# Four weight combinations prepared five rounds later, and three engines' work reordered at the start of a fused retention and mixture kernel

## The chip, the cores and the metric

The kernel runs on one core of a Trainium2 chip. The metric is the device time of one execution in microseconds (us). Engines: PE (matrix products), DVE (vector), ACT (scalar and copies), POOL (GpSimd, elementwise here) and SP, whose queue issues nearly all transfers.

## The reference, cut to what matters

```python
def _attn_ref(q, k, v):                    # B, H, S, D = 4, 8, 768, 64
    gamma = 1.0 - 2.0 ** (-5.0 - np.arange(H, dtype=np.float32))
    for t in range(S):
        state = gamma[None, :, None, None] * state + np.einsum('bhd,bhe->bhde', k[:, :, t], v[:, :, t])
        y[:, :, t] = scale * np.einsum('bhd,bhde->bhe', q[:, :, t], state)

def _moe_ref(x, domain_probs, w1, w2):     # N, D, E, F = 3072, 512, 4, 1024
    p = domain_probs / (domain_probs.sum(-1, keepdims=True) + 1e-09)
    for e in range(E):
        h = np.maximum(x @ w1[e], 0.0)
        out += p[:, e:e + 1] * (h @ w2[e])
```

All values are float32. The output of the retention, 768 tokens of 512 columns for each of four batches, is the input x of four experts, whose results are added with normalised weights p.

## The kernel before, in words

**Numbers in two parts.** A float32 factor of a product is held as a high part (a rounded copy in the type fp32r, made by ACT: `w1h`, `xh`, `hh`, `c2h`, `w2h`) and a low part (the factor minus its high part, made by DVE or POOL: `w1l`, `xl`, `hl`, `c2l`, `w2l`). A product is then three products on PE: high by high, high by low, low by high.

**Rounds.** The experts' hidden columns are worked off in 16 rounds for each batch (n = 0 to 15 for the first one, 64 in all). A round multiplies x by a 512x256 piece of w1. From n = 1 on it does so with seven products of half-size blocks in place of eight, in the order `SEQ = (1, 5, 6, 2, 7, 3, 4)`; this needs sums and differences of blocks of x (`t1`, `t2`, `t4`, and the block b12 of `xr`, which is overwritten) and of w1. The seven blocks of w1 lie in one tile, `w1h` and `w1l`: part 0 holds three raw blocks (columns 0 to 2), part 1 four combinations (columns 3 to 6, made by `combine_w1` in the tile `s`). The products collect in the banks ps_x, ps_y and ps_z; ACT copies intermediate sums out (`u`), DVE adds them (L434), ACT and DVE make the two parts of the relu (`hh`, `hl`, L448 and L449).

**Round 0** is done differently: `whole` (L541) multiplies plain blocks, with the three raw blocks of w1 in part 0 and the fourth one (`a21`, `a` in the profile). So the combinations of w1[0] are not used in round 0. They are used by the later batches, which fetch all seven blocks of each round from DRAM (`kept1`, stored by `save_w1`).

**The second product.** For the first batch p2 (L561) multiplies hidden values by w2, into two banks ps_o, which ACT empties in round 0 (L578) and DVE later (L580). For the other batches w2 is also combined (`combine_w2`, which overwrites the loaded tile `w2r`, giving `c2h` and `c2l`) and kept in DRAM. `w2r` is one tile: the load of the next w2 (L270) has to wait until the last reader, c2l, is done.

**The order is written out by hand**: each engine executes its instructions in the order of the code. The opening runs the six chunks of the first attention (L707 to L739), then the four `whole` products with the preparation of x and of round 1's weights between them (L740 to L777). Then comes the loop over rounds n and their seven products k = 0 to 6 (L781 on): at each k come product p1(n, i), one p2 of the round before, and `weights(n, k)` (L354), which prepares weights for round n + 1. In that function k = 0 does c2h of the round before and starts `combine_w1` of the next one on POOL, k = 1 does c2l and loads the next w2, k = 4 and 5 make w2h and w2l, k = 6 combines w2 on POOL. The steps of the next batch's attention are spread through the rounds. Tiles with few buffers tie the queues together: `w1r` has two, `s`, `w2r`, ps_y and ps_z one each.

Of the kernel before, what the change touches and what calls it, by code (L numbers as in the profile page):

```python
# [7 lines left out]
F32 = mybir.dt.float32  # L8
F32R = mybir.dt.float32r
ACTF = mybir.ActivationFunctionType  # L10
ALU = mybir.AluOpType
# [13 lines left out]
WARM = (384, 384, 384, 384)  # L25
NB0 = S // 128
NP = NRND // 2
ATT_STEPS = 2 * NCHB + 2


# [30 lines left out]
def retention_moe(ctx: ExitStack, tc: tile.TileContext, qk, kv, w1, w2, probs, probt, cst, cqs, out, out_t):  # L61
# [260 lines left out]
        eng.tensor_tensor(out=a12, in0=a12, in1=a11, op=ALU.subtract)  # L322

    def save_w1(n):
        for i, x in enumerate(wt1[n]):
            nc.sync.dma_start(out=kept1[n][:, :, i, :], in_=x.bitcast(F32))

    def save_w2(n, d, at, which=(0, 1), eng=None):
        for i in which:
# [24 lines left out]
    def weights(n, k):  # L354

        m = n + 1
        if k == 0:
            if n == 1:
                save_w1(1)
                x_lo(0, 4)  # L360
            hi2(n - 1, wc2, "c2")
            if m < NRND:
                load_w1(m + 1)
                combine_w1(m, nc.gpsimd)
                w1_hi(m, 0)
        elif k == 1:
            lo2(n - 1, wc2, nc.vector)
            load_w2(n)
            if m < NRND:
                w1_lo(m, 0, nc.gpsimd)  # L370
        elif k == 2:
            save_w2(n - 1, wc2, 4)
            if n == 3:
                gates()
        elif k == 3 and m < NRND:
            w1_hi(m, 1)
        elif k == 4:
            hi2(n, wt2, "w2")
            if m < NRND:
                w1_lo(m, 1, nc.gpsimd)  # L380
        elif k == 5:
            lo2(n, wt2, nc.vector if m < NRND else nc.gpsimd)
            if m < NRND:
                save_w1(m)
        elif k == 6:
            combine_w2(n, nc.gpsimd)
            if m < NRND:
                save_w2(n, wt2, 0)
            else:
                save_w2(n, wt2, 0, (0,), nc.scalar)  # L390
# [290 lines left out]
    with tc.manual_schedule():  # L681
# [25 lines left out]
        for ci in range(NCHB):  # L707
# [8 lines left out]
            if ci == 1:  # L716
                w1_hi(0, 0)
                first_a21(0)
                combine_w1(0, nc.gpsimd)
            elif ci == 2:  # L720
                w1_hi(0, 1)
                w1_lo(0, 0, nc.gpsimd)
            elif ci == 3:
                for i in SEQ:
                    x_tiles(0, i)
                for i in (1, 2):
                    x_hi(0, i)
                first_a21(1)
                first_gates()
            elif ci == 4:  # L730
                decay(ci + 1)
                w1_lo(0, 1, nc.gpsimd)
                w1_hi(1, 0)
                hi2(0, wt2, "w2")
                load_w1(2)
                load_qk(6)
                load_kv(6)
# [1 line left out]
                decay(ci + 1)  # L739
        start[0] = False  # L740
        early, late = slice(0, 2 * C), slice(2 * C, HB)
        x_lo(0, 1, eng=nc.gpsimd)
        for i in (7, 3):
            x_hi(0, i, early)
        x_lo(0, 7, early, nc.gpsimd)
# [5 lines left out]
            x_lo(0, i, late)  # L751
        combine_w1(1, nc.gpsimd)
        whole(*WHOLE[0])
        w1_hi(1, 1)
        w1_lo(1, 1, nc.gpsimd)
        w1_lo(1, 0, nc.gpsimd)
        for c in range(2):
            combine_x(0, c, nc.vector, None, 0)
        whole(*WHOLE[1])
        lo2(0, wt2, nc.vector)  # L760
        combine_x(0, 2, nc.vector, None, 0)
        x_hi(0, 5)
        whole(*WHOLE[2])
        x_hi(0, 6)
        x_lo(0, 5)
        whole(*WHOLE[3])
        x_lo(0, 6)
        for c in range(3):
            combine_x(0, c, None, nc.gpsimd, 1)
        for i in range(3):  # L770
            p2(0, i)
        for i in (7, 4):
            x_hi(0, i)
        x_lo(0, 7, eng=nc.gpsimd)
        combine_w2(0, nc.gpsimd)
        save_w1(0)
        save_w2(0, wt2, 0)  # L777

# [129 lines left out]
```

## Time and profile before

| what | value |
|---|---|
| device time, median of 3 runs | 1063.77 us (1063.53 to 1064.26) |
| profiled execution | 1063.8 us, of it the profile's span 1062.0 us |
| busy in the span | PE 98%, DVE 67%, POOL 64%, ACT 36% |
| mean granted clock of PE | 0.996 |
| HBM traffic over the span | 274 GB/s (read 221.64 MB, written 69.26 MB) |

Times in the profile count from the start of the span. A row of the timeline gives start, length, engine, line, operation, output<-inputs, shape, and in brackets how long the engine had been idle and what released it. SPq rows are the issue of a transfer by SP. The name `k` stands for tiles in DRAM.

### The profile page before, as it was taken

How to read it: one execution, taken by the hardware profiler on the slowest of the kernel's cores; microseconds unless marked ns; L12 is line 12 of the kernel's file. 1: busy time of each engine (PE TensorE's matmuls, PEld its weight loads, DVE VectorE, ACT ScalarE, POOL GpSimd, SP SyncE). 2: the span in 40 equal slices, each digit the busy share in tenths (PEclk: the TensorE clock that was granted, in tenths of full speed). 3: DMA queues.
4: the chain of work that ended last, by engine and by line, in shares of the span. 5: the costliest groups of instructions: out<-in, count | busy, mean ns of one | idle time of the engine just before them, and what ended most of it. 6: DMA issues, size and time to landing. Idle time of an engine off the chain costs nothing.

```text
span 1062.0 us, 18481 instructions
## 1 busy us (share of the span) xinstructions
PE 1045.1 (98%) x6714; PEld 993.7 (94%) x6714; DVE 713.6 (67%) x1181; ACT 379.1 (36%) x728; POOL 678.4 (64%) x643
## 2 busy tenths in 40 slices
PE   8889999999999999999999999999999999999998
PEld 6778888888888999999999999999999999999998
DVE  5757767667766467677588467667679746677664
ACT  2354333344444422322252532332234443323320
POOL 5977675866757664655579754655658865555561
PEclk9999999999999999999999999999999999999999
DMA  9689999998979777878778987877678887787873
GB/s 343 227 287 331 352 298 331 299 335 274 363 253 333 256 259 262 269 269 279 243 246 270 327 278 242 263 265 268 225 253 261 292 288 260 251 268 252 264 263 103
DMA packets 153883, 292.13 MB, mean 275 GB/s; under 512 B 12352, under 2 KB 76992, under 8 KB 153792
## 3 DMA queue, kind: packets, MB, share of 16 engines
q1 hardware_dynamic: 151872, 288.32, 81.0%
q10 hardware_dynamic: 1920, 2.62, 0.7%
q8 instruction: 54, 0.88, 0.3%
q14 instruction: 37, 0.30, 0.1%
HBM read 221.64 MB, written 69.26 MB: 274 GB/s over the span
## 4 chain that ended last, share of the span: by engine, by line
PE 88%; DVE 3%; POOL 3%; DMA 2%; issue 2%; ACT 2%; POOLq 0%; DVEq 0%; ACTq 0%
PE ps_u L598 31%; PE ps_x L521 23%; PE ps_z L521 12%; PE ps_o L572 9%; PE ps_y L521 6%; PE ps_s L149 2%; PE ps_v L196 2%; PE ps_u L617 1%; POOL xl L253 1%; DMA w1r<-in_w 1%; PE ps_v L190 1%; PE ps_v L163 1%; DMA w2r<-in_w 1%; DVE w2l L314 0%; DVE ol L461 0%
## 5 line engine op out<-in xcount | busy, mean ns | idle before, releaser
L598 PE MATMUL ps_u<-oh,v 128*128 128x384 f32 x1288 | 378.9, 334 | 0.3 <-DVE sum L434 0.3
L472 POOL TENSOR_TENSOR b<-b 128x384 f32<-128x384 f32 x184 | 196.3, 1067 | 176.7 <-DVE b L470 150.7
L434 DVE TENSOR_TENSOR sum<-ps_u,sum 128x384 f32<-128x384 f32 x288 | 158.3, 550 | 135.7 <-PE ps_u L598 122.6
L598 PEld LDWEIGHTS ps_u<-oh,v 128*128 128x128 f32 x1288 | 237.2, 188 | 1.0 <-DVE sum L434 0.7
L461 POOL TENSOR_TENSOR ol<-b,oh 128x384 fp32r<-128x384 f32 x188 | 197.7, 1070 | 61.3 <-ACT oh L456 55.1
L456 ACT ACTIVATE oh<-b 128x384 fp32r<-128x384 f32 x330 | 160.6, 518 | 208.0 <-DVE b L470 111.2
L521 PE MATMUL ps_x<-xh,v 128*128 128x384 f32 x768 | 227.5, 337 | 0.2
L598 PE MATMUL ps_u<-ol,v 128*128 128x384 f32 x644 | 215.2, 334 | 0.0
L428 ACT ACTIVATE u<-ps_x 128x384 f32<-128x384 f32 x126 | 61.8, 490 | 253.1 <-PE ps_x L521 252.1
L461 DVE TENSOR_TENSOR ol<-b,oh 128x384 fp32r<-128x384 f32 x142 | 130.2, 917 | 25.6 <-ACT oh L456 25.6
L521 PEld LDWEIGHTS ps_x<-xh,v 128*128 128x128 f32 x768 | 141.4, 188 | 3.0 <-ACT u L428 0.9
L521 PE MATMUL ps_x<-xl,v 128*128 128x384 f32 x384 | 128.4, 334 | 0.0
L598 PEld LDWEIGHTS ps_u<-ol,v 128*128 128x128 f32 x644 | 120.9, 188 | 0.0
L521 PE MATMUL ps_z<-xh,v 128*128 128x384 f32 x384 | 113.9, 337 | 1.2 <-DVE ol L461 1.2
L580 DVE SCALAR_TENSOR_TENSOR acc<-ps_o,pm,acc 128x512 f32<-128x512 f32 x90 | 67.0, 744 | 38.4 <-PE ps_o L572 38.3
L572 PE MATMUL ps_o<-w2h,hh 128*128 128x512 f32 x192 | 75.6, 394 | 5.1 <-ACT acc L578 5.1
L572 PE MATMUL ps_o<-w2h,hl 128*128 128x512 f32 x192 | 76.1, 396 | 0.0
L572 PE MATMUL ps_o<-w2l,hh 128*128 128x512 f32 x192 | 76.0, 396 | 0.0
L521 PEld LDWEIGHTS ps_z<-xh,v 128*128 128x128 f32 x384 | 70.7, 188 | 2.4 <-DVE b L470 1.5
L521 PEld LDWEIGHTS ps_x<-xl,v 128*128 128x128 f32 x384 | 72.1, 188 | 0.1
L521 PE MATMUL ps_z<-xl,v 128*128 128x384 f32 x192 | 64.2, 334 | 0.0
L521 PE MATMUL ps_y<-xh,v 128*128 128x384 f32 x192 | 56.9, 337 | 0.0
(123 smaller groups left out, 1663.8 us busy)
## 6 DMA issues: line engine op xcount, KB each, us to landing
v<-k SPq DMA_DIRECT2D x336, 256.0 KB, 3.2
v<-k SPq DMA_DIRECT2D x165, 512.0 KB, 4.2
k<-w1h SPq DMA_DIRECT2D x16, 896.0 KB, 7.0
k<-w1l SPq DMA_DIRECT2D x16, 896.0 KB, 7.0
qk<-in_qk SPq DMA_DIRECT2D x24, 512.0 KB, 5.4
kv<-in_kv SPq DMA_DIRECT2D x24, 512.0 KB, 5.8
w1r<-in_w SPq DMA_DIRECT2D x16, 512.0 KB, 7.0
w2r<-in_w SPq DMA_DIRECT2D x16, 512.0 KB, 4.3
```

Source lines behind the costliest of these rows:

```text
L149: nc.tensor.matmul(ps[r][:, p, :], lhsT=a[rows, 1, p, :], rhs=a[rows, 0, p, :], start=True, stop=True)
L163: nc.tensor.matmul(y[64 * r:64 * r + 64, p, :], lhsT=v[:, 0, h, :], rhs=v[:, 1, h, :], start=(bank is None), stop=True, skip_group_check=True,
L196: nc.tensor.matmul(ps[r][64 * k:64 * k + 64, half, :], lhsT=v[:, 1, h, :], rhs=sp[:, h, :], start=(c == 0 and half == 0), stop=True, skip_ ...
L428: nc.scalar.activation(out=t, in_=ps, func=ACTF.Copy)
L434: nc.vector.tensor_tensor(out=o, in0=ps, in1=u, op=ALU.add)
L456: nc.scalar.activation(out=hi, in_=t, func=ACTF.Copy)
L461: eng.tensor_tensor(out=lo, in0=t, in1=hi.bitcast(F32), op=ALU.subtract)
L472: sub = lambda o, a, b: nc.gpsimd.tensor_tensor(out=o, in0=a, in1=b, op=ALU.subtract)
L521: nc.tensor.matmul(ps, lhsT=lhsT[:, cs], rhs=rhs[:, kt, :], start=(fresh and m == 0), stop=(m == 5), skip_group_check=True,)
L572: nc.tensor.matmul(ps, lhsT=a[:, ts], rhs=b[:, fs, :], start=(m == 0), stop=(m == 5))
L580: nc.vector.scalar_tensor_tensor(out=acc[nt], in0=ps, scalar=sc, in1=acc[nt], op0=ALU.mult, op1=ALU.add)
L598: nc.tensor.matmul(ps, lhsT=w[:, r, l, ds], rhs=o, start=(m == 0), stop=(m == 5))
```

## The change

Five things are moved, and nothing is computed differently.

1. The combinations of w1[0] (four POOL operations), their high part on ACT and their low part on POOL leave the opening. `save_w1(0)` stores only the three raw blocks. In round `REST` = 5 w1[0] is loaded again (k = 2), combined on POOL (k = 5), and `rest_w1` (k = 6) makes the two parts block by block (ACT copy, POOL subtraction) and stores each. For the buffer that this takes, the load of w1[8] moves from k = 0 to k = 3 of round 6.
2. x1's low part moves on POOL from behind the attention to the place that the low part of w1[0]'s combinations had.
3. The first w2 low part moves from DVE to POOL, its combinations from POOL to DVE.
4. The second high part of x7 and that of x4 on ACT, the low part of x7 on POOL and the first c2h move from the end of the opening into round 1, k = 0 and 1.
5. The high and low parts of w1[1]'s combinations, and of t1 and t2 (x5, x6), are put behind later products; the first two p2 are issued ahead of x5's and x6's high parts.

Line numbers in the rows below differ by a few between the two kernels, as the change adds lines.

POOL at the end of the first attention and in what follows it, before (`yst` is the decay of the attention's state, `xl` a low part of x, `s` a combination of w1):

```order
L175 TENSOR_TENSOR yst_113<-yst_113,cst 128x256
L295 TENSOR_TENSOR w1l<-s,w1h 128x1024
L253 TENSOR_TENSOR xl<-xr,xh 128x768
L253 TENSOR_TENSOR xl<-xr,xh 128x2x256
L278 TENSOR_TENSOR s<-w1r 128x256
L279 TENSOR_TENSOR s<-s,w1r 128x256
L280 TENSOR_TENSOR s<-w1r,s 128x256
L281 TENSOR_TENSOR s<-w1r 128x256
L295 TENSOR_TENSOR w1l<-s,w1h 128x1024
L295 TENSOR_TENSOR w1l<-w1r,w1h 128x768
L222 TENSOR_TENSOR xr<-xr 128x2x128
```

and of the change:

```order
L176 TENSOR_TENSOR yst_113<-yst_113,cst 128x256
L254 TENSOR_TENSOR xl<-xr,xh 128x768
L254 TENSOR_TENSOR xl<-xr,xh 128x2x256
L279 TENSOR_TENSOR s<-w1r 128x256
L280 TENSOR_TENSOR s<-s,w1r 128x256
L281 TENSOR_TENSOR s<-w1r,s 128x256
L282 TENSOR_TENSOR s<-w1r 128x256
L315 TENSOR_TENSOR w2l<-w2r,w2h 128x1024
L296 TENSOR_TENSOR w1l<-s,w1h 128x1024
L296 TENSOR_TENSOR w1l<-w1r,w1h 128x768
L223 TENSOR_TENSOR xr<-xr 128x2x128
```

x1's low part follows the last decay directly; w2's low part of 1024 columns has come in between the combinations of w1[1] and their low parts.

ACT from the first p2 into round 1, before (`acc` empties a bank of p2, `xh<-t` and `xh<-xr` are high parts of x5, x6, x4 and x7, `u` empties a bank of p1):

```order
L249 ACTIVATE xh<-t_521 128x768
L448 ACTIVATE hh<-ps_h 128x384
L578 ACTIVATE acc<-ps_o,pm 128x512 x3
L249 ACTIVATE xh<-xr 128x768
L249 ACTIVATE xh<-t_522 128x768
L428 ACTIVATE u<-ps_x 128x384
L310 ACTIVATE c2h<-w2r 128x1024
L290 ACTIVATE w1h<-w1r 128x768
L428 ACTIVATE u<-ps_z 128x384
L578 ACTIVATE acc<-ps_o,pm 128x512
L428 ACTIVATE u<-ps_x 128x384
```

and of the change:

```order
L604 ACTIVATE acc<-ps_o,pm 128x512
L250 ACTIVATE xh<-t_512 128x768
L604 ACTIVATE acc<-ps_o,pm 128x512
L454 ACTIVATE u<-ps_x 128x384
L250 ACTIVATE xh<-xr 128x768
L291 ACTIVATE w1h<-w1r 128x768
L454 ACTIVATE u<-ps_z 128x384
L604 ACTIVATE acc<-ps_o,pm 128x512
L250 ACTIVATE xh<-t_513 128x768
L311 ACTIVATE c2h<-w2r 128x1024
L454 ACTIVATE u<-ps_x 128x384
```

c2h has moved behind the next round's part of w1h, a copy `u`, an `acc` and x4's high part, and x7's and x4's high parts behind the first `u`.

POOL at the end of round 5 and the start of round 6, of the change (before, `w2r` follows `w1l<-s` directly):

```order
L296 TENSOR_TENSOR w1l<-s,w1h 128x1024
L279 TENSOR_TENSOR s<-w1r 128x256
L280 TENSOR_TENSOR s<-s,w1r 128x256
L281 TENSOR_TENSOR s<-w1r,s 128x256
L282 TENSOR_TENSOR s<-w1r 128x256
L335 TENSOR_TENSOR w1c<-s,w1c 128x256 x4
L320 TENSOR_TENSOR w2r<-w2r 128x256
L321 TENSOR_TENSOR w2r<-w2r 128x256
L322 TENSOR_TENSOR w2r<-w2r 128x256
L323 TENSOR_TENSOR w2r<-w2r 128x256
```

Eight operations stand ahead of w2's combinations there. On ACT the four copies stand ahead of the first `u` of round 6; on SP the new load stands behind the store of c2l of round 5.

The diff:

```diff
     def save_w1(n):
+        p = slice(0, 7 if n else 3)
         for i, x in enumerate(wt1[n]):
-            nc.sync.dma_start(out=kept1[n][:, :, i, :], in_=x.bitcast(F32))
+            nc.sync.dma_start(out=kept1[n][:, p, i, :], in_=x[:, p].bitcast(F32))
+
+    def rest_w1():
+
+        for i in range(4):
+            t, u = v1_p.tile([128, 2, 256], F32R, tag="v1", name="w1c"), comb1[0][:, i, :]
+            nc.scalar.activation(out=t[:, 0, :], in_=u, func=ACTF.Copy)
+            nc.gpsimd.tensor_tensor(out=t[:, 1, :], in0=u, in1=t[:, 0, :].bitcast(F32), op=ALU.subtract)
+            nc.sync.dma_start(out=kept1[0][:, 3 + i], in_=t.bitcast(F32))
...
@@ weights(n, k), m = n + 1
         if k == 0:
             if n == 1:
                 save_w1(1)
-                x_lo(0, 4)
-            hi2(n - 1, wc2, "c2")
+                x_hi(0, 7)
+                x_lo(0, 7, eng=nc.gpsimd)
+                combine_w2(0, nc.vector)
+            if n > 1:
+                hi2(n - 1, wc2, "c2")
             if m < NRND:
-                load_w1(m + 1)
+                if n != REST + 1:
+                    load_w1(m + 1)
                 combine_w1(m, nc.gpsimd)
                 w1_hi(m, 0)
         elif k == 1:
+            if n == 1:
+                x_hi(0, 4)
+                x_lo(0, 4)
+                hi2(0, wc2, "c2")
             lo2(n - 1, wc2, nc.vector)
...
+            elif n == REST:
+                load_w1(0)
         elif k == 3 and m < NRND:
             w1_hi(m, 1)
+            if n == REST + 1:
+                load_w1(m + 1)
...
             if m < NRND:
                 save_w1(m)
+            if n == REST:
+                combine_w1(0, nc.gpsimd)
         elif k == 6:
+            if n == REST:
+                rest_w1()
             combine_w2(n, nc.gpsimd)
...
@@ the first attention, chunk ci
             if ci == 1:
                 w1_hi(0, 0)
                 first_a21(0)
-                combine_w1(0, nc.gpsimd)
             elif ci == 2:
-                w1_hi(0, 1)
                 w1_lo(0, 0, nc.gpsimd)
...
             elif ci == 4:
                 decay(ci + 1)
-                w1_lo(0, 1, nc.gpsimd)
+                x_lo(0, 1, eng=nc.gpsimd)
...
@@ behind the attention
-        x_lo(0, 1, eng=nc.gpsimd)
         for i in (7, 3):
             x_hi(0, i, early)
...
         combine_w1(1, nc.gpsimd)
         whole(*WHOLE[0])
+        lo2(0, wt2, nc.gpsimd)
+        for c in range(2):
+            combine_x(0, c, nc.vector, None, 0)
+        whole(*WHOLE[1])
         w1_hi(1, 1)
         w1_lo(1, 1, nc.gpsimd)
         w1_lo(1, 0, nc.gpsimd)
-        for c in range(2):
-            combine_x(0, c, nc.vector, None, 0)
-        whole(*WHOLE[1])
-        lo2(0, wt2, nc.vector)
         combine_x(0, 2, nc.vector, None, 0)
+        whole(*WHOLE[2])
+        whole(*WHOLE[3])
+        p2(0, 0)
         x_hi(0, 5)
-        whole(*WHOLE[2])
+        x_lo(0, 5)
+        p2(0, 1)
         x_hi(0, 6)
-        x_lo(0, 5)
-        whole(*WHOLE[3])
         x_lo(0, 6)
         for c in range(3):
             combine_x(0, c, None, nc.gpsimd, 1)
-        for i in range(3):
-            p2(0, i)
-        for i in (7, 4):
-            x_hi(0, i)
-        x_lo(0, 7, eng=nc.gpsimd)
-        combine_w2(0, nc.gpsimd)
+        p2(0, 2)
         save_w1(0)
         save_w2(0, wt2, 0)
```

More of the change, by code (lines that the diff above doesn't have):

```diff
@@ L27 @@
 NP = NRND // 2
+REST = 5
 ATT_STEPS = 2 * NCHB + 2
```

## The prediction, on record before the changed kernel ran

> **What bounds the kernel now.** I read the page's busy times first, then the busy time by stage, then what TensorE (PE) waited for, then each engine's rows in order of time between 20 and 70 us and around 115 to 145 us.
>
> ```profile
> PE 1045.1 (98%) x6714; PEld 993.7 (94%) x6714; DVE 713.6 (67%) x1181; ACT 379.1 (36%) x728; POOL 678.4 (64%) x643
> ...
> 20.00:30.00 10.00, 7.47 (x141) 5.97 (x137) 9.53 (x19) 5.16 (x8) 9.20 (x9) 1.00 0.89 302
> 30.00:40.00 10.00, 9.80 (x47) 9.80 (x48) 8.40 (x11) 1.98 (x3) 8.67 (x8) 0.83 0.61 215
> 40.00:50.00 10.00, 8.02 (x39) 6.63 (x38) 7.05 (x7) 6.03 (x10) 9.48 (x9) 1.00 0.91 288
> 50.00:60.00 10.00, 6.90 (x29) 5.90 (x28) 3.31 (x4) 5.12 (x9) 9.13 (x10) 0.88 0.22 46
> 60.00:70.00 10.00, 10.00 (x61) 9.14 (x61) 5.70 (x9) 4.26 (x7) 7.04 (x8) 0.95 1.06 367
> ```
>
> The columns are the stretch, its length, and the busy time of PE, its weight load, DVE, ACT and POOL, then the granted clock, DMA share and GB/s. PE is busy 98% of the span, and from 60 us on without a gap. Its own order is not changed by the edit, so it gains only by entering the steady rounds earlier, and loses only where it is made to stop. Of its 17 us without work, 7.8 us lie between 20 and 60 us, and there the clock is at 0.83 and 0.88 in two of the four stretches.
>
> ```profile
> PE ps_o L572 <- ACT acc L578: 5.1, 2, 3.1
> PE ps_h L555 <- POOL xl L253: 2.6, 1, 2.6
> PE ps_v L190 <- POOL yst L175: 1.1, 1, 1.1
> ...
> 30.20 0.64 PE L555 MATMUL ps_h<-xl,w1h 128*128 128x384 f32 x1 [2.63 <-POOL xl L253]
> 44.98 0.50 PE L572 MATMUL ps_o<-w2h,hh 128*128 128x512 f32 x1 [1.98 <-ACT acc L578]
> 56.71 0.50 PE L572 MATMUL ps_o<-w2h,hh 128*128 128x512 f32 x1 [3.10 <-ACT acc L578]
> 65.24 0.33 PE L521 MATMUL ps_z<-xh,w1h 128*128 128x384 f32 x1
> ...
> 31.00:32.00 1.00, 1.00 (x5) 1.00 (x4) 1.00 (x1) 0.00 (x0) 1.00 (x2) 0.50 1.09 381
> 59.00:60.00 1.00, 1.00 (x4) 1.00 (x4) 0.00 (x0) 1.00 (x2) 0.52 (x1) 0.50 0.73 280
> ```
>
> These are PE's waits (total, times, longest), four PE rows (start, length, in brackets the wait and what ended it) and two stretches of 1 us. PE waits 2.6 us for the low part of x1 from POOL, then 2.0 and 3.1 us for a bank that ACT empties. After the waits of 2.6 and 3.1 us the clock is at 0.50. A mean of 0.83 over 30 to 40 us is 3.4 us at half speed, and so are 0.88 and 0.95 over 50 to 70 us together: each costs PE 1.7 us more. After the wait of 2.0 us the clock stays up.
>
> What sets the end of this opening is the queue of POOL, and behind it a chain through w2:
>
> ```profile
> 26.92 1.13 ACT L249 ACTIVATE xh<-xr 128x512 fp32r<-128x512 f32 x2
> 27.63 4.20 POOL L253 TENSOR_TENSOR xl<-xr,xh 128x768 fp32r<-128x768 f32 x2
> 36.25 2.66 POOL L295 TENSOR_TENSOR w1l<-s,w1h 128x1024 fp32r<-128x1024 f32 x1 [1.17 <-ACT w1h L290]
> 45.50 1.45 POOL L222 TENSOR_TENSOR xr<-xr 128x256 f32<-128x256 f32 x1
> 47.26 0.84 ACT L249 ACTIVATE xh<-xr 128x768 fp32r<-128x768 f32 x1
> 53.91 1.06 ACT L310 ACTIVATE c2h<-w2r 128x1024 fp32r<-128x1024 f32 x1 [4.70 <-POOL w2r L322]
> 54.88 0.83 ACT L290 ACTIVATE w1h<-w1r 128x768 fp32r<-128x768 f32 x1
> 55.61 0.47 ACT L428 ACTIVATE u<-ps_z 128x384 f32<-128x384 f32 x1
> 55.98 0.68 ACT L578 ACTIVATE acc<-ps_o,pm 128x512 f32<-128x512 f32 x1
> 55.00 1.45 DVE L314 TENSOR_TENSOR c2l<-w2r,c2h 128x1024 fp32r<-128x1024 f32 x1 [4.17 <-ACT c2h L310]
> 56.48 0.35 SPq L270 DMA_DIRECT2D w2r<-in_w  x1
> 62.74 1.06 ACT L310 ACTIVATE w2h<-w2r 128x1024 fp32r<-128x1024 f32 x1 [0.71 <-DMA w2r<-in_w]
> 64.21 0.56 DVE L449 SCALAR_TENSOR_TENSOR hl<-ps_z,hh 128x384 fp32r<-128x384 f32 x1 [1.11 <-ACT hh L448]
> ```
>
> The third subtraction into b12 (xr<-xr) on POOL ends at 45.50 + 1.45 = 46.95, and ACT's second high part of x7 follows at 47.26. c2h waits 4.7 us for POOL's w2 combinations; its low part c2l ends at 56.45. Then w2r may be overwritten: the next load is issued at 56.48, its high part starts at 62.74. On ACT the relu of ps_z stands behind that high part, so hl<-ps_z ends at 64.77, and only then may the second product of round 2 write ps_z. PE does that at 65.24 without a wait.
>
> **The change, term by term.** Seen from the profiled execution of 1063.8 us (span 1062.0; the median of the three runs is 1063.77, so I use one for the other).
>
> *The attention.* POOL loses the four combinations of w1[0], which made PE's 1.1 us wait at ps_v; what is late next there are loads, which do not move. Between nothing and 1.1 us I take 0.8. x1's low part loses the low part of 1024 columns ahead of it (2.40 us by the row at 125.46 below) and these 0.8, so it ends near 27 or sooner and not as PE starts at 30.20. The wait of 2.6 us and its halved clock go, and PE ends the four whole products 4 to 5 us earlier.
>
> *That is not carried through.* POOL's long run begins with x7's early low part, which waits for ACT's high part. That is the first of the two in the row at 26.92, and it ends at 27.5; it stands behind a w1 load that does not move. Of old the run began when x1's low part ended, at 30.2, and reached 46.95 with one wait of 1.17 us: 15.6 us of work. New in it is w2's low part.
>
> ```profile
> 310.76 2.41 POOL c2l L314
> 34.98 0.41 DVE L222 TENSOR_TENSOR t<-xr 128x256 f32<-128x256 f32 x1
> 39.91 2.06 DVE L222 TENSOR_TENSOR t<-xr 128x256 f32<-128x256 f32 x1
> ```
>
> The first row is a subtraction of the same size that POOL does late in the program (2.41 us). So x7's second high part can start at 27.5 + 15.6 + 2.4 + 0.3 (the step from 46.95 to 47.26) = 45.8 instead of 47.26. PE, which came early, gives back some 1.5 us where round 1 needs w1[1]'s second low part from this same run. The other two rows are one DVE operation on 128x256 with POOL idle and with POOL busy: 0.41 and 2.06 us. The four w2 combinations, never seen on DVE, cost there 4 x 0.41 = 1.6 to 4 x 2.06 = 8.2 us; I take 3, nearer to the idle row, since POOL was slower beside such work but seldom by much (2.66 for 2.40 at 36.25). They follow x6's low part, and ACT wants them 3 us after x7, so they hide unless they take over 8 us. Their cost to POOL lies between nothing and their own 1.6 us; I take 0.2, as DVE also loses a low part: 46.0.
>
> From there ACT's new order has no hole, and by the starts of its rows above: x7 0.74, w1's next high part 0.73, u 0.37, acc 0.57, x4 0.74, c2h 1.06, 50.2 in all. DVE adds c2l, 1.45, and some 0.3 for x4's low part ahead of it: **52.0 instead of 56.45**. The 4.7 us in which ACT waited for POOL are most of the gain. Bounds: 50.8, if the rows of 2.66 and 1.45 on POOL shrink to 2.40 and 0.74, and 53.6, if one operation on DVE is held up as the row of 2.06 was.
>
> The way from c2l to the free ps_z bank is a load and the same order on ACT and DVE as before: 64.77 - 56.45 = 8.3 us. So the second product of round 2 starts at 60.4 and not at 65.24: **4.9 us earlier**. PE is there before: the last product of round 1 waits for the sum into ps_c, behind c2l and four steps of half a microsecond on DVE and ACT (54.2), then come that product and the first of round 2, at most 1.25 us each: 56.5. PE then stands still for some 4 us, longer than either wait after which the clock was halved, so I charge **1.7 us**. Net: 3.2 us.
>
> *Round 5.* Added are a load of 512 KB, four copies on ACT, eight POOL operations and four stores of 256 KB. The first save of w1 is 1 MB smaller, off the path.
>
> ```profile
> 21.60 0.73 POOL L306 TENSOR_TENSOR a<-w1r,a 128x256 fp32r<-128x256 f32 x1
> 121.72 0.50 SPq L330 DMA_DIRECT2D k<-c2l  x1
> k<-c2l SPq DMA_DIRECT2D x1, 512.0 KB, 6.9
> DMA to landing us min/median/max: 4.2/7.0/10.2
> 122.08 1.83 POOL L295 TENSOR_TENSOR w1l<-w1r,w1h 128x768 fp32r<-128x768 f32 x1
> 125.46 2.40 POOL L295 TENSOR_TENSOR w1l<-s,w1h 128x1024 fp32r<-128x1024 f32 x1
> 131.98 0.74 POOL L319 TENSOR_TENSOR w2r<-w2r 128x256 f32<-128x256 f32 x1 [4.12 <-DVE w2l L314]
> 135.19 1.06 ACT L310 ACTIVATE c2h<-w2r 128x1024 fp32r<-128x1024 f32 x1 [1.46 <-POOL w2r L322]
> 142.53 1.25 PE ps_x L521 x6
> ```
>
> In times of before: the new load waits on its buffer for w1's low part (122.08 + 1.83 = 123.9) and stands behind the store of c2l, issued at 121.72 with 6.9 us to landing: 128.6. 512 KB at the 381 GB/s of the stretch at 31 us are 1.4 us more: it lands at 130.0. (The row of all w1 loads, 4.2 to 10.2 us with a median of 7.0, would give 128.1 to 134.1 and 130.9.) POOL, free at 127.86, waits for it, combines to 133.4, subtracts to 136.6 (eight operations of 0.73 with gaps) and ends w2's combinations at 139.9 instead of 135.1. The copies on ACT run beside that. ACT then does c2h, the next w1 part and two u by 142.5. The product that overwrites the bank of the second u stands on PE at 142.53, since the attention's products lie ahead of it there. POOL's idle 4.1 us ahead of 131.98 and this slack are the cover, and they just do; I charge 0.2 us. Beyond it, each microsecond that the load is late is one on PE. On SP the stores of the copies hold up w2's stores to 136.6, and the later load of w1[8] the next qk load; both are read most of a round later.
>
> Sum: -4.9 + 1.7 + 0.2 = **-3.0 us**, 1060.8.
>
> **The rivals.** *The clock is not halved* (0.21). The halving came after waits of 2.6 and 3.1 us, but not after 2.0 us; a wait cut into two by a product or shortened to 2.5 us escapes it. Then -4.7: 1059.1. Against it, 4 us is longer than both. The Trainium skill, "TensorE: Matmul & The Clock Gate", Part 1, has the clock judged in free-running windows of about 3.4 us; by that rule a wait of 4.1 us that straddles two windows can leave both half busy and unpunished, which would give this time. The two halved stretches here, 3.4 us each, agree with the window's length.
>
> *DVE and POOL slow each other more* (0.22). The whole opening runs on both, and both now do two-operand work on SBUF side by side. The POOL subtraction of 1.45 us at 45.50, against 0.74 at 131.98 for the same size, shows the price: if each of the four DVE combinations costs POOL 0.4 us and not 0.05, x7's high part is back at 47.4, c2l at 53.4, and the gain is 4.9 - 1.4 - 1.7 - 0.2 = 1.6: 1062.2, within the noise. The Trainium skill, "SBUF — State Buffer", Who interferes with whom, has DVE's second SBUF input and POOL's reads share one port as an exclusive lock, which speaks against moving these four to DVE; by it POOL would lose their whole 1.6 us. The trace agrees only in part: the POOL row at 36.25 lost 0.26 us, the one at 45.50 0.71.
>
> *The reload comes late* (0.12), the one that ends slower. From 130.0 on each microsecond stops PE at round 6's product of 142.53, and from 2.6 us on the clock is halved as well. Landing at 133.6 costs 3.6 + 1.7 = 5.3, and the sum is -3.2 + 5.3 = +2.1: 1065.9; that is where it decides. The row of 10.2 us allows it; the median of 7.0 and what stands in the queue speak against it.
>
> **How the numbers follow.** My forecast has 0.45 and spans 1059.5 to 1062.3 by the bounds of c2l. A measurement of this kernel can tell about 0.2%, 2.1 us, from no change, so faster means below 1061.7: three quarters of the forecast (0.34) and the first rival (0.21): 0.55. The rest of the forecast and the second rival are the same: 0.33. Slower: 0.12. The range goes from the first rival with c2l at 50.8 (1057.9, taken down to 1057.6 for the attention) to a reload at 132.7, which costs 2.7 + 1.7 and eats more than the gain (1065.0).
>
> **What would show it.** Right: no wait at the first ps_h, the clock at 1.00 around 31; POOL's xr subtractions ending near 46; c2l ending near 52; PE's longest wait before ps_z of round 2, some 4 us, freed by hl; one halved stretch after 60. In round 5 POOL waits for w1r to land and PE has no wait at round 6's ps_x. Wrong: c2l at 54 or later, a second halved stretch, or a wait of PE behind ACT's u in round 6. My sum fails most easily in how long POOL and DVE hold each other up.

## The result, and the profile after

| | median (range, runs) | profiled execution | span |
|---|---|---|---|
| before | 1064.01 us (1063.53 to 1065.49, 4) | 1063.8 us | 1062.0 us |
| after | 1057.63 us (1057.32 to 1057.91, 4) | 1057.9 us | 1056.0 us |

The ratio is 0.9938 (95% interval 0.9923 to 0.9953): 6.4 us faster by the medians, 5.9 by the two profiled executions. The prediction had 3.0 us and a range down to 1057.6.

The page of the kernel after (busy time, share, instructions), and then PE's waits in it (total, times, longest):

```profile
PE 1043.6 (99%) x6714; PEld 991.6 (94%) x6714; DVE 714.4 (68%) x1184; ACT 380.1 (36%) x731; POOL 680.8 (64%) x643
```

```profile
PE ps_o L598 <- DVE hl L475: 2.1, 1, 2.1
...
PE ps_z L547 <- DVE hl L475: 1.0, 1, 1.0
PE ps_x L547 <- ACT u L454: 0.4, 1, 0.4
```

The two old causes, POOL's low part of x1 and ACT's emptying of ps_o (7.7 us together), are gone from the list. In their place stand 2.1 us for hl at ps_o, a wait that the forecast did not have, and 1.0 us at ps_z, where the forecast had some 4. By stage (length, busy time of PE, its weight load, DVE, ACT and POOL, granted clock, DMA share, GB/s) the kernel after shows:

```profile
30.00:40.00 10.00, 7.93 (x41) 6.99 (x40) 9.93 (x9) 3.12 (x5) 9.84 (x8) 0.98 0.61 207
40.00:50.00 10.00, 10.00 (x44) 8.72 (x43) 9.86 (x11) 7.70 (x11) 9.77 (x10) 0.85 0.52 162
50.00:60.00 10.00, 8.99 (x58) 7.96 (x57) 7.13 (x11) 5.73 (x11) 8.47 (x6) 1.00 0.71 227
60.00:70.00 10.00, 10.00 (x51) 8.90 (x50) 6.76 (x11) 4.50 (x7) 9.61 (x10) 1.00 1.05 358
...
41.00:42.00 1.00, 1.00 (x4) 0.81 (x3) 1.00 (x3) 0.88 (x2) 1.00 (x2) 0.50 1.01 346
```

A mean of 0.98 and then 0.85 is 3.4 us at half clock, 1.7 us of work lost; it lies near 41 us, and none lies after 50. The three other executions of the kernel after have a mean clock of 1.000, so they had no such stretch, and took 1057.32 to 1057.79 us: at most 0.6 us less than the profiled one, not 1.7. The rows that answer to the chain of the prediction, in the order of the chain, are these:

```profile
43.58 1.45 POOL L223 TENSOR_TENSOR xr<-xr 128x256 f32<-128x256 f32 x1
45.06 0.85 ACT L250 ACTIVATE xh<-xr 128x768 fp32r<-128x768 f32 x1
49.10 1.06 ACT L311 ACTIVATE c2h<-w2r 128x1024 fp32r<-128x1024 f32 x1 [0.70 <-DVE w2r L323]
50.41 1.75 DVE L315 TENSOR_TENSOR c2l<-w2r,c2h 128x1024 fp32r<-128x1024 f32 x1
52.19 0.35 SPq L271 DMA_DIRECT2D w2r<-in_w  x1
56.19 1.06 ACT L311 ACTIVATE w2h<-w2r 128x1024 fp32r<-128x1024 f32 x1 [1.12 <-DMA w2r<-in_w]
57.66 0.56 DVE L475 SCALAR_TENSOR_TENSOR hl<-ps_z,hh 128x384 fp32r<-128x384 f32 x1 [1.53 <-ACT hh L474]
58.28 0.44 PE L547 MATMUL ps_z<-xh,w1h 128*128 128x384 f32 x1 [1.01 <-DVE hl L475]
```

c2l ends at 52.16 (forecast 52.0), but the second product of round 2 starts at 58.28 and not at 60.4. It is 6.96 us earlier than before (65.24): 4.29 of it come from c2l (56.45 before), 2.26 from the way from c2l to the end of hl (8.32 before, 6.06 now), and 0.41 because PE now follows hl at once. Both kernels run the same 6714 products in the same order, so each can be compared with itself: PE of the kernel after stays 6.9 us ahead up to 129 us and is 6.0 ahead from 143 us on. Round 6 thus takes 0.9 back, 0.4 of it as a wait at ps_x and the rest in smaller delays, and 0.1 goes elsewhere: 6.0 us of span.

### The profile page after: what moved, and what is told of

Same layout as the page of the kernel before. It is cut to its first block, busy times and chain, and to the rows that moved or that the text cites. A ratio compares the mean times of both kernels' runs of the same rounds, so it can differ in the third digit from the quotient of the medians.

```text
span 1056.0 us, 18496 instructions
## 1 busy us (share of the span) xinstructions
PE 1043.6 (99%) x6714; PEld 991.6 (94%) x6714; DVE 714.4 (68%) x1184; ACT 380.1 (36%) x731; POOL 680.8 (64%) x643
## 4 chain that ended last, share of the span: by engine, by line
PE 87%; DVE 5%; DMA 2%; POOL 2%; issue 2%; ACT 1%; SPq 0%; POOLq 0%; DVEq 0%; ACTq 0%
PE ps_u L624 31%; PE ps_x L547 23%; PE ps_z L547 12%; PE ps_o L598 9%; PE ps_y L547 6%; PE ps_s L150 2%; PE ps_v L197 2%; PE ps_u L643 1%; DMA w2r<-in_w 1%; DMA kv<-in_kv 1%; DVE t L223 1%; PE ps_v L191 1%; DVE xl L254 1%; POOL xl L254 1%; PE ps_v L164 0%
## 5 line engine op out<-in xcount | busy, mean ns | idle before, releaser
L487 DVE TENSOR_TENSOR ol<-b,oh 128x384 fp32r<-128x384 f32 x142 | 128.0, 901 | 25.7 <-ACT oh L482 25.7
```

What stands on the lines that cost most here:

```text
L487: eng.tensor_tensor(out=lo, in0=t, in1=hi.bitcast(F32), op=ALU.subtract)
```

## The experiments

Theory A, formed on this result: the chain c2l, load of w2r, w2h, hh, hl, ps_z sets when PE enters the steady rounds. Its rivals: POOL's long queue sets it; the reload of round 5 takes a part of the gain back; the load was not on the path. Line numbers differ by a few from kernel to kernel. Each ratio below is to runs of the kernel before made in the same session on the same chip; their medians differ by 1.0 us between sessions (1063.34 to 1064.32), so smaller differences between medians of different sessions say little.

**Where does the load's time come from?** The load of w2[1] took 6.2 us to landing before and 4.0 after. Three runs ask why.

*Behind the stores:* on the kernel after, with the two stores of c2 ahead of the load on SP.

```diff
         elif k == 1:
             lo2(n - 1, wc2, nc.vector)
+            if n == 1:
+                save_w2(0, wc2, 4)
             load_w2(n)
```

> The changed kernel with one thing moved: in round 1 the two stores of c2h and c2l (1 MB) are issued ahead of the load of the next w2 and not behind it. Theory A (the load decides: in the changed kernel it took 4.0 us from issue to ACT's high part against 6.3 before, and that with a clock not halved is why the gain was twice the forecast): the load lands some 2.5 us later, PE waits 3 to 4 us at ps_z of round 2 instead of 1.0, and that wait is followed by a halved stretch: 1060 to 1062 us. Theory B (the gain came from the opening up to 57 us, and this load has slack): 1057.5 to 1058.5 us.

Measured: 1059.59 us (1057.97 to 1063.28, 10 runs), ratio 0.9961 (0.9949 to 0.9972); profiled 1057.97. One store waits for c2h only, so the load was issued just 0.15 us later and landed in 4.6 us.

```profile
59.06 0.44 PE L550 MATMUL ps_z<-xh,w1h 128*128 128x384 f32 x1 [2.46 <-DVE hl L478]
```

ps_z moved by 0.8 us with the load, as the chain has it. No halved stretch followed the wait of 2.46 us. The profiled time hardly moved and the median rose by 2, over a wide spread: too weak to price the load, and between the two theories. The profiled execution is the only one of the ten with a mean clock of 1.000 (the others have 0.995 to 0.998), so the others had halved stretches that it lacks.

*Fewer columns, more instructions ahead of the attention:* the trace has in the load of before one packet of 16 KB in the queue for instructions. On the kernel before, 26 products in place of four move that packet.

```diff
-WARM = (384, 384, 384, 384)
+WARM = (384, 128) + (32,) * 24
```

> The kernel before with more and smaller warming products at its start (26 in place of 4, about the same time in all), so that PE's stream is some 88 instructions longer ahead of everything. Theory A1 (the load of w2 that took 6.3 us from issue to ACT's high part was slow because a block of instructions of 16 KB was fetched in it, 2.9 us against about 1 elsewhere): the fetch moves to about 50 us and that load takes 4 to 4.8 us. Rival A2 (it was slow because the DMA queues had been idle before it): still 5.8 to 6.5 us. The time stays at 1063 to 1065 us by both, since PE did not wait for this load.

Measured: 1067.6 us (one run). The packet came 6.6 us ahead of the load, and the load took 4.2 us. But these products took 12.2 us in place of 5.3, so all else was shifted too. A smaller dose keeps their length:

```diff
-WARM = (384, 384, 384, 384)
+WARM = (384,) + (32,) * 9
```

> The kernel before, with ten products ahead of the attention in place of four, nine of them 32 columns wide, so that these take about as long (5 us) but PE has six instructions more. It tells whether the packet of instructions that lay in the load of w2[1] in the kernel before (2.9 us, from 57.9) is what made that load take 6.2 us. By the theory that it is: the packet comes several microseconds earlier, ahead of the load's issue near 56.5, and the load takes 4.0 to 4.4 us. By the rival (the load was long for another reason, such as the stores behind it): it takes 5.5 to 6.5 us wherever the packet is. The time hardly moves either way (1063 to 1065), since PE reached ps_z of round 2 without a wait before: the load was not what held it there.

Measured: 1061.64 us (one run). The transfers in the 6 us behind the load's issue, before (packets, MB and share of the 16 DMA engines for a queue; KB and us to landing for an issue), and the same load in the run, which has no such packet beside it:

```profile
q8 instruction: 1, 0.02, 3.1%
...
w2r<-in_w SPq DMA_DIRECT2D x1, 512.0 KB, 6.2
```

```profile
w2r<-in_w SPq DMA_DIRECT2D x1, 512.0 KB, 3.9
```

3.1% of 16 engines and 6 us is one packet that held one engine for 2.9 us. With the packet gone from there, and stores, order and size as before, the load takes 3.9 us. So the packet is what made the load of before long, and the rival (the stores behind it) falls. Of its size less is settled: with part 1 alone (below) a packet of 1.4 us lay late in the load, which took 5.8; with ACT's order put back one of 1.3 us lay near its start, and it took 4.4. In eleven kernels, those of these two runs among them, none lay in it and it took 3.9 to 4.6 us. A packet is not the only way to a long load: the next run's took 6.0 us without one, behind a store. The time, which was to stay at 1063 to 1065, came out lower, in a single run: PE's second wait for ACT was 2.2 us and not 3.1, no halved stretch followed it (one followed the first, of 2.1 us), and ps_z of round 2 started at 63.92 in place of 65.24.

**Is the load on the path, and is a long wait halved?** On the kernel after, the load is issued 3 us later, behind the store of round 2's high parts.

```diff
         elif k == 1:
-            load_w2(n)
+            if n > 1:
+                load_w2(n)
...
         elif k == 3 and m < NRND:
             w1_hi(m, 1)
+            if n == 1:
+                nc.sync.dma_start(out=kept1[m][:, :, 0, :], in_=wt1[m][0].bitcast(F32))
+                load_w2(n)
```

> The kernel after, with the load of w2[1] issued on SP behind the store of round 2's high parts of w1, near 55.2 instead of 52.2, and nothing else moved on any engine. This makes the wait that the forecast had: PE ready near 57.3, ps_z free near 61.3. Theory A: each microsecond of the load's delay is one on PE, so ps_z of round 2 starts 2.8 to 3.2 us later, with a wait of about 4 us freed by hl. Of the clock: by the forecast the wait is followed by a halved stretch of 3.4 us within 3 us, 1.7 us more: in all +4.5 to +4.9, profiled 1062.4 to 1062.8. Rival (a wait of 4 us may miss both windows): +2.8 to +3.2, profiled 1060.7 to 1061.1. Rival (the load is not on the path): within 1 us of 1057.9.

Measured: 1064.51 us (1063.6 to 1065.42, 11 runs), ratio 1.0005 (0.9996 to 1.0014), the whole gain lost; profiled 1064.06. Its rows and stretches of 2 us:

```profile
61.17 1.06 ACT L311 ACTIVATE w2h<-w2r 128x1024 fp32r<-128x1024 f32 x1 [6.20 <-DMA w2r<-in_w]
63.25 0.69 PE L553 MATMUL ps_z<-xh,w1h 128*128 128x384 f32 x1 [6.07 <-DVE hl L481]
```

```profile
62.00:64.00 2.00, 0.75 (x2) 0.75 (x3) 1.36 (x2) 1.37 (x4) 0.00 (x0) 0.50 1.09 379
64.00:66.00 2.00, 2.00 (x7) 1.91 (x7) 1.99 (x4) 0.00 (x0) 1.46 (x2) 0.50 1.05 382
66.00:68.00 2.00, 2.00 (x9) 1.69 (x9) 0.36 (x1) 0.34 (x1) 1.84 (x4) 0.78 1.06 288
```

The load was 3.0 us late and took 2.0 us longer behind the 896 KB of the store; ps_z came 4.97 us later, and PE then worked at half clock up to about 66.6, 1.7 us more. 4.97 + 1.7 = 6.7, against 6.2 by the profiles and 6.9 by the medians. So the load stood on the path microsecond for microsecond, and the forecast's price of 1.7 us for a long wait at this place was right for a wait of 6.1 us; one of 4 us did not come up here.

**Which parts of the change carry it?** Part 1 alone on the kernel before (attention, round 5 and save as in the change, all else old):

> The kernel before with part 1 of the change alone: w1[0]'s combinations made in round 5, nothing else moved. Theory A: POOL's run starts 2.7 us earlier, the first wait of 2.6 us and its halved stretch go, but ACT still waits for w2's combinations on POOL and PE for ACT's two banks, so the chain ends 2.5 us earlier and round 5 takes 0.4 us back: 1061 to 1062.5 us. Theory E (the removed POOL work is the whole of it): 1057 to 1058.5 us.

Measured: 1061.97 us (1059.67 to 1063.63, 10 runs), ratio 0.9986 (0.9976 to 0.9995). PE still waits twice for ACT:

```profile
41.88 0.79 PE L591 MATMUL ps_o<-w2h,hh 128*128 128x512 f32 x1 [2.13 <-ACT acc L597]
54.87 0.51 PE L591 MATMUL ps_o<-w2h,hh 128*128 128x512 f32 x1 [2.86 <-ACT acc L597]
```

The change without part 1 (the combinations of w1[0] back in the attention, no reload, x1's low part behind them):

```diff
+                combine_w1(0, nc.gpsimd)
             elif ci == 2:
+                w1_hi(0, 1)
...
+                w1_lo(0, 1, nc.gpsimd)
                 x_lo(0, 1, eng=nc.gpsimd)
```

> The changed kernel without part 1: w1[0]'s combinations are back in the opening, nothing is done for them in round 5, all else is as changed. Theory A: POOL's run starts 2.5 us later, c2l ends near 54.7, PE waits 3 to 4 us at ps_z of round 2 with a halved stretch behind it, and 0.4 us of round 5 is won: 1059.5 to 1061.5 us. Theory E (part 1 is the whole of it): 1063 us or more. Theory F (parts 2 to 5 are the whole of it): 1057 to 1058 us.

Measured: 1061.17 us (1059.14 to 1062.36, 10 runs), ratio 0.9977 (0.9967 to 0.9988). The first wait of before is back, and 6.8 us at half clock with it (from 29.6). The time is that of theory A, but not its wait: at ps_z of round 2 PE waited 1.8 us, not 3 to 4, and no stretch was halved behind it.

```profile
30.39 0.69 PE L581 MATMUL ps_h<-xl,w1h 128*128 128x384 f32 x1 [2.62 <-POOL xl L254]
```

The ratios less 1 are 0.14% and 0.23% by themselves, 0.62% together. Each half leaves one of the two old causes of PE's waits standing; c2l ended at 54.6 and 54.9, and only both bring it to 52.2.

Without the reload of round 5:

> The changed kernel without the reload of w1[0], its combinations and the ACT copies and POOL subtractions of round 5; the combinations of w1[6] are stored in their place, so later batches use other values for four blocks of that round. Theory A (round 5 is covered by POOL's idle time but for PE's one wait of 0.4 us): 0.3 to 0.6 us faster than the changed kernel, 1057.0 to 1057.4 us. Theory C (the round 5 work costs PE more than that one wait, through the queues behind it): 1.5 us or more faster, under 1056.2 us.

Measured: 1057.74 us (1057.19 to 1057.81, 4 runs), ratio 0.9947 (0.9931 to 0.9964). The medians show no cost of the reload and its 16 operations, but they cannot tell it: the runs of either kernel spread by 0.6 us. The profiled time, 1057.19, is 0.7 us below that of the kernel after, and the rows show where. First ACT and PE in round 6 of the kernel after, then the same two rows of this run:

```profile
133.59 1.06 ACT L311 ACTIVATE c2h<-w2r 128x1024 fp32r<-128x1024 f32 x1 [5.13 <-POOL w2r L323]
136.20 0.44 PE L547 MATMUL ps_x<-xh,w1h 128*128 128x384 f32 x1 [0.40 <-ACT u L454]
```

```profile
128.32 1.06 ACT L311 ACTIVATE c2h<-w2r 128x1024 fp32r<-128x1024 f32 x1 [1.46 <-POOL w2r L323]
135.59 0.44 PE L541 MATMUL ps_x<-xh,w1h 128*128 128x384 f32 x1
```

With the eight operations ahead of w2's combinations on POOL, ACT gets to c2h 5.3 us later, its copies u behind that come late as well, and PE waits for the second. Compared product by product with the kernel before, PE loses 0.9 us between 129 and 143 us in the kernel after and nothing in this run. The change without part 1, which has no reload either, loses nothing there, and the nine other runs that have it lose 0.4 to 0.8 us. So the reload costs PE 0.9 us in round 6 of the kernel after. That is more than theory A had, but the profiled time is in its band, because this run loses 0.2 us more than the kernel after at the start of the next batch.

Part 3 undone (w2's first low part on DVE, its combinations on POOL), and part 4 undone (x7, x4 and c2h in ACT's old order):

```diff
-        lo2(0, wt2, nc.gpsimd)
+        lo2(0, wt2, nc.vector)
...
-                combine_w2(0, nc.vector)
+                combine_w2(0, nc.gpsimd)
```

> The changed kernel with w2's first low part back on DVE and its combinations back on POOL, behind x7's low part. Theory A (chain c2h, c2l, load, ps_z): POOL is 2.6 us shorter up to x7's high part but then has 3.3 us of combinations ahead of c2h, so c2h starts within 1.5 us of its 49.1 and the time is 1057 to 1059.5 us. Theory D (taking w2's combinations off POOL is what gave the gain, since ACT had waited 4.7 us there): c2h starts at 52 or later, 1061 us or more.

```diff
         p2(0, 2)
+        for i in (7, 4):
+            x_hi(0, i)
+        x_lo(0, 7, eng=nc.gpsimd)
...
             if n == 1:
-                x_hi(0, 4)
-                x_lo(0, 4)
-                hi2(0, wc2, "c2")
...
```

> The changed kernel with part 4 undone: ACT's second high parts of x7 and of x4 ahead of the first u, and c2h directly behind u, as before. Theory A: u, the second u and the emptying of p2's bank come 2 us later behind x4's high part and c2h, PE waits for them as it did before (up to 3 us, with a halved stretch if over 2), while c2l itself ends within 1 us of 52.2: 1058.5 to 1061 us. Rival G (ACT's order matters little, since the chain to ps_z is what sets the time): 1057.3 to 1058.2 us.

Measured, part 3 undone: 1059.88 us (1058.34 to 1060.85, 5 runs), ratio 0.9963 (0.995 to 0.9976), 2.2 us slower than the change by the medians and 0.4 by the profiled executions:

```profile
50.83 1.06 ACT L311 ACTIVATE c2h<-w2r 128x1024 fp32r<-128x1024 f32 x1 [3.25 <-POOL w2r L323]
52.32 0.44 PE L547 MATMUL ps_x<-xh,w1h 128*128 128x384 f32 x1 [3.28 <-ACT u L454]
```

ACT again waits for POOL's combinations, PE for the copy behind it on ACT. c2h starts 1.7 us later than in the change, between theories A and D. The run with only w2's low part on DVE (below) differs from this one in the combinations alone: 1056.91 us for 1059.88 by the medians, 1055.83 for 1058.34 profiled. So taking them off POOL is worth 2.5 to 3.0 us there. Part 4 undone: 1058.72 us (1057.55 to 1059.3, 7 runs), ratio 0.9958 (0.9946 to 0.997); c2l ended where it did. That is 1.1 us above the change by the medians and 0.4 below it by the profiled executions, and the intervals of the ratios overlap: what part 4 is worth stays open.

**What holds PE now, and is there more?** First, the parts of w2[1] behind both relus of round 1, so that hl does not need the load:

```diff
         elif k == 4:
-            hi2(n, wt2, "w2")
+            if n > 1:
+                hi2(n, wt2, "w2")
...
         elif k == 6:
+            if n == 1:
+                hi2(1, wt2, "w2")
+                lo2(1, wt2, nc.vector)
```

> The kernel after, with the high and low part of w2[1] issued behind the two relus of round 1 (k = 6) instead of ahead of them (k = 4). Theory A (what still sets the time of the opening is the chain c2l, load of w2r, w2h on ACT, hh, hl, ps_z of round 2): with w2h behind the relu, hl<-ps_z needs the load no more. The sum into ps_z on DVE ended at 56.13 in the profile after, so hl ends near 57.2, PE arrives at 57.27, the wait of 1.0 us ahead of ps_z goes, and ps_z starts near 57.3. Time 0.6 to 1.0 us under that of the kernel after: profiled 1056.9 to 1057.3. Rival B (the load only happened to land then; hl is held up by something else as well): the wait moves to another row, w2l or w1l of round 2, and the time stays within 0.3 us of 1057.9.

Measured: 1058.52 us (1057.5 to 1058.96, 5 runs), ratio 0.9947 (0.9935 to 0.996): the mechanism of rival B, though the time lies 0.6 us above 1057.9 and not within 0.3. The wait at ps_z went and came back 2 us further on, for the low part of the same load:

```profile
60.13 0.50 PE L603 MATMUL ps_o<-w2l,hh 128*128 128x512 f32 x1 [1.24 <-DVE w2l L315]
```

Second, w2's first low part on DVE while the combinations stay there too (the first hunk of part 3 undone, above):

> The kernel after, with only the first w2 low part back on DVE; the combinations of w2 stay on DVE too, so POOL has 2.5 us less in its long run. Theory A: POOL's last subtraction into xr ends near 42.5 instead of 45.0, its low part of round 2's combinations near 54.7 instead of 57.2; DVE has 1.5 us more but is blocked by one POOL operation less, so c2l ends between 50 and 52. The wait of 1.0 us ahead of ps_z stays within 1 us of that, because it hangs on c2l and the load and not on POOL's queue: profiled 1057 to 1058.5. Rival C (POOL's queue is what sets the end of the opening): ps_z of round 2 starts 2 us earlier, 1055.5 to 1056. Rival D (DVE becomes the bound): c2l at 53 or later, 1059 or more. On DVE blocked by POOL: the t operations of 2.6 and 2.5 us in the profile after lay beside POOL's w2l and w1l; here only one long one should be left, and the wait of PE of 2.1 us should shrink below 1.

Measured: 1056.91 us (1055.83 to 1057.8, 5 runs), ratio 0.9934 (0.9922 to 0.9947), the lowest of all; profiled 1055.83. POOL's queue is shorter, c2l ends at 50.98, the wait of 2.1 us at ps_o and its halved stretch are gone:

```profile
34.30 0.42 DVE L223 TENSOR_TENSOR t<-xr 128x256 f32<-128x256 f32 x1
35.57 2.16 DVE L223 TENSOR_TENSOR t<-xr 128x256 f32<-128x256 f32 x1
57.29 0.44 PE L547 MATMUL ps_z<-xh,w1h 128*128 128x384 f32 x1 [1.63 <-DVE hl L475]
```

The chain is that of theory A, and the profiled time that of rival C, but not by its mechanism: ps_z came 1.0 us earlier, not 2. The rest of the 2.1 us came later: PE lost 0.5 us less in round 6 and 0.5 less at the start of the next batch.

Third, both edits, and fourth, the second with only w2h moved, between the two relus:

> The two edits of the last two runs together: w2[1]'s parts behind the relus of round 1, and the first w2 low part on DVE. Theory A: with the load chain off the path, what stands next is POOL's low part of round 2's combinations (57.2 in the profile after, 54.7 without w2l on POOL) and PE's own arrival (57.3, of it 2.1 us of waiting and 1.7 us of halved clock near 40). So ps_z of round 2 starts between 55 and 56.5 instead of 58.3: 1.8 to 3.3 us under the kernel after, profiled 1054.6 to 1056.1, and more than either edit alone. Rival C (POOL's queue alone): the same as the run with w2l on DVE. Rival B: within 0.5 us of the kernel after.

> The kernel after, with the first w2 low part on DVE (as in the run of that edit alone, which is the best so far) and the high part of w2[1] issued on ACT between the two relus of round 1 (k = 5), its low part where it was. In the run with both parts behind both relus the wait of 1.6 us ahead of ps_z shrank to 0.5, but PE then waited 1.2 us for w2l. Theory A (the chain of c2l, load, w2h and the relu of ps_z set the last wait): now ps_z of round 2 starts near 56.0 and w2l ends near 57.6, as PE wants it, so both waits are under 0.5 us, and the time is 0.8 to 1.3 us under that of w2l on DVE alone: profiled 1054.5 to 1055.0, if no stretch is halved. Rival (something else holds PE by as much, POOL's low part of round 2's combinations near 56.4 or the second relu): the wait moves to it, 1055.5 to 1056.5.

Measured: 1058.0 us (1056.74 to 1058.66, 5 runs), ratio 0.9943 (0.9931 to 0.9956), and 1057.48 us (1056.44 to 1057.82, 5 runs), ratio 0.9934 (0.992 to 0.9947). PE in the first, and PE and DVE in the second:

```profile
55.99 0.45 PE L552 MATMUL ps_z<-xh,w1h 128*128 128x384 f32 x1 [0.46 <-DVE hl L480]
58.78 0.64 PE L603 MATMUL ps_o<-w2l,hh 128*128 128x512 f32 x1 [1.22 <-DVE w2l L315]
```

```profile
55.85 0.45 PE L550 MATMUL ps_z<-xh,w1h 128*128 128x384 f32 x1 [0.44 <-DVE hl L478]
56.18 2.04 DVE L315 TENSOR_TENSOR w2l<-w2r,w2h 128x1024 fp32r<-128x1024 f32 x1 [0.39 <-ACT w2h L311]
58.27 0.50 PE L601 MATMUL ps_o<-w2l,hh 128*128 128x512 f32 x1 [0.87 <-DVE w2l L315]
```

ps_z started where theory A put it (56.0, 55.9), but the sum did not follow. w2l took 2.04 us beside POOL in the second and PE waited for it in both, and in the first a halved stretch followed (59 to 62.4). In the fourth run no stretch was halved, and still its profiled time, 1057.5, is no better: later waits of PE, for the first loads of the next batch (1.4 us at ps_z, 0.8 in the second run) and for the copy in round 6 (0.4), take back what the opening gave. No version measured here is faster than the change by more than the intervals; w2's low part on DVE is 0.7 us below it by the medians and 2.1 by the profiles.

## Why the prediction was wrong in size

- *The attention*: right. No wait at the first ps_h, the clock at 1.00 around 31, PE past the four whole products 4.9 us earlier (its first ps_o at 35.14 for 40.06), as the term had it.
- *POOL's run and ACT's hole*: right in the sum. x7's second high part started at 45.06 for 46.0, but DVE's four combinations took 4.6 us for my 3, c2h waited 0.70 for them, and c2l ended at 52.16 for 52.0. So the combinations did not hide, as I had said of anything under 8 us, and the early x7 made up for that: the two errors cancel, which is luck. The two runs with w2's first low part on DVE, one with the combinations on POOL and one on DVE, show that ACT no longer waiting for POOL is worth 2.5 to 3.0 us.
- *"The way from c2l to the free ps_z bank is a load and the same order on ACT and DVE as before: 8.3 us"*: this is the first step that failed, by 2.3 us. The order was the same, the load was not: 4.0 us for 6.2. Its length was taken from one execution in which a packet of instructions happened to lie in it. In the kernel after that packet came near 49, ahead of the load, and the run with the packet alone moved shows 3.9 us. The warning stood on the page of before, whose median over the 16 loads is 4.3 us:

```profile
w2r<-in_w SPq DMA_DIRECT2D x16, 512.0 KB, 4.3
```

- *"PE then stands still for some 4 us ... so I charge 1.7 us"*: the second step that failed. The price was right for the wait of 6.1 us of the late load; the wait of 4 us was not there. PE came at 57.27, not 56.5, and ps_z was free at 58.22, not near 60.4: 1.0 us. A halved stretch did come, behind the unforeseen wait at 38.60, but at a place where PE had later to wait anyhow, so it cost little: the executions without it were at most 0.6 us faster. The rival "the clock is not halved" comes nearer in time (1059.1), but not by its mechanism, which keeps the long wait.
- *"POOL's idle 4.1 us ahead of 131.98 and this slack are the cover, and they just do; I charge 0.2 us"*: the third step that failed, by 0.7 us and to the other side. POOL waited for the new load, as forecast (2.7 us for 2.1). The load landed 6.6 us after its issue, at 123.70, which is 130.6 in times of before (6.9 us more) and not 130.0, and each microsecond beyond the cover was to be one on PE. c2h started at 133.59 (140.5 in times of before, forecast 139.9), and PE lost 0.9 us, 0.4 of it behind ACT's u in round 6. That wait stood among my signs of being wrong. The row of POOL's wait:

```profile
123.70 0.75 POOL L279 TENSOR_TENSOR s<-w1r 128x256 f32<-128x256 f32 x1 [2.70 <-DMA w1r<-in_w]
```

- The sum of -3.0 less 2.1 (ps_z) and 1.7 (the clock) is -6.8; with 0.9 in round 6 for the 0.2 charged, and 0.1 elsewhere, it is the span's -6.0.
- *The range*: the measured 1057.63 lies inside it by 0.03 us, and that is luck. Its lower end was built from c2l at 50.8 and no halved stretch, with 0.3 for the attention. c2l ended at 52.16, and the difference came from the load, which the range held fixed.
- *DVE and POOL slow each other more*: the rival was real, but it fell on DVE and not on the chain. In the kernel after:

```profile
32.70 2.58 POOL L315 TENSOR_TENSOR w2l<-w2r,w2h 128x1024 fp32r<-128x1024 f32 x1
35.24 2.56 POOL L296 TENSOR_TENSOR w1l<-s,w1h 128x1024 fp32r<-128x1024 f32 x1
...
32.95 2.62 DVE L223 TENSOR_TENSOR t<-xr 128x256 f32<-128x256 f32 x1
35.60 2.48 DVE L223 TENSOR_TENSOR t<-xr,t 128x256 f32<-128x256 f32 x1
38.00 0.54 DVE L475 SCALAR_TENSOR_TENSOR hl<-ps_h,hh 128x384 fp32r<-128x384 f32 x1
...
38.60 0.50 PE L598 MATMUL ps_o<-w2h,hl 128*128 128x512 f32 x1 [2.07 <-DVE hl L475]
```

Each DVE operation of 0.41 us that started inside a long POOL operation ended 0.3 us after it, while POOL lost some 0.2 us of 2.6. The two make hl late, and PE waits for it. With w2l on DVE the t operations of that place took 0.42 us and PE's wait at ps_o was gone; the one beside POOL's remaining low part still took 2.16. The Trainium skill, "SBUF — State Buffer", Who interferes with whom, says that whoever of the two issues first gets the shared pair of ports for the whole instruction. The rows agree; I had set the rule aside because the POOL rows of before lost little, and did not ask what it does to the DVE operation that starts second.

## What to carry to other kernels

A duration of a transfer taken from one row of one execution is the least safe term of a sum: compare it with the same transfer in other rounds, and look at what else lay in its queues there. Where two engines share a port, a long operation of the one is a wait of its whole length for a short one of the other, and that wait travels to whatever is queued behind the short one. An early halving of the clock cost next to nothing here, because PE had to wait for something else later; price it only where PE sets the pace up to the end. Work put into a later round is not free because an engine idles there: follow what it delays to the next wait of PE (0.9 us here), and look for that in the rows, since runs that spread by 0.6 us do not show it.

## What the runs showed of the hardware that was not expected

- A 16 KB packet of instructions in the load of 512 KB went with 5.8 and 6.2 us to landing in place of 3.9 to 4.6, though it held one DMA engine for only 1.4 and 2.9 us; one at the start of the load went with 4.4.
- After a wait of 2.07 us (kernel after) PE was at half clock for 3.4 us, after one of 2.46 us (load behind the stores) and of 1.98 us (before) it was not; after 6.07 us it was. In the run with the packet alone moved it was after 2.14 us and not after 2.53. In the three other executions of the kernel after the clock was at 1.000 throughout, with the same program. The Trainium skill, "TensorE: Matmul & The Clock Gate", Part 1, has the clock judged in free-running windows of about 3.4 us, which agrees with the lengths and with the chance in it; that a window must be idle as a whole does not agree with 2.07 us.
- A few short products ahead of the attention, which change no other work, moved both the packet and the halved stretches; that run's 1061.64 us lie 2.2 us under the profiled execution of before.
